# Two mixture-of-experts layers behind a long convolution: two second-layer sums to a PSUM bank, a third table of slots, and another order of items

## The chip, the cores and the metric

The kernel runs on one NeuronCore of a Trainium2 chip. The metric is the device time of one execution in microseconds; the median of three runs before the change is 1368.7 (1364.27 to 1370.17). TensorE is called PE, its weight loads PEld, VectorE DVE, ScalarE ACT, GpSimd POOL, and SyncE SP, whose queue issues most plain DMAs. DMAs with an index per row (gathers and scatters) are issued on POOL.

## The reference

```python
X = np.fft.rfft(x, axis=1)                       # x: 4 x 2496 x 256
y = np.fft.irfft(X * (filt_r + 1j * filt_i), n=2496, axis=1)
# layer 1: x = y as 9984 tokens of 256; 8 experts, 1248 tokens each
logits = x @ w_gate
# tokens and experts are paired greedily, best logit first, until an expert is full
h = np.maximum(x[mask] @ w1[e], 0.0); out[mask] = h @ w2[e]      # 256 -> 1024 -> 256
# layer 2: x = out; cosine similarity to 8 expert embeddings over tau
logits = xn @ en.T / tau
expert_idx = np.argmax(logits, axis=1)           # any number of tokens per expert
gate_w = softmax(logits)[expert_idx]
out[mask] = gate_w[mask, None] * (np.maximum(x[mask] @ w1[e], 0.0) @ w2[e])
```

## The kernel before

The convolution fills the first 250 us or so and leaves the tokens in DRAM (`xs`) and the first gate's logits in SBUF. From there on the kernel is one list of items (`plan`, line 1418), worked through by `layers` (line 1548).

An item is up to 512 tokens of one expert, in tiles of 128. Its columns are transposed on PE (L995) during the item before, at that item's fourth and sixth chunk of eight. The first matmuls (`l1`, L1012) run in eight chunks of 128 hidden columns, six matmuls each, since every operand is split into a high and a low part: ACT takes the high part of a sum (`k_hh`, L1015), DVE the rest (`k_hl`, L1018). The second matmuls (`l2`) follow two chunks behind. Weights are loaded on SP's queue (L940, L950), ACT rounds them to the high part and DVE or POOL subtracts for the low part (L957, L958); `engs` of a set says which of the two.

There are first-layer items and second-layer items ("slots"). First-layer items come in groups: the first full expert, then seven "known" experts in four groups, then seven "late" ones in three groups, a late item being the last 480 tokens of an expert. The greedy pairing (`search`), the lists of tokens (`listing`) and the routing of each finished group (`routes`) run as generators beside the matmuls. A group's `route` computes the second gate for its tiles (square sums on ACT, Newton steps on POOL, the rest on DVE and one small pair of matmuls, L1376 and L1377) and scatters the rows (the tiles `k_y`, 26 buffers in all) by POOL into `ys`, a DRAM region per second-layer expert.

A slot is 512 rows of one expert's region in `ys`. Which expert and which rows are in a table computed on DVE: `slA` (8 slots, only whole ones) when the last known group is routed, `slB` (12 slots) and `slS` (2 half slots) when all are. Behind the last table `pads` writes padding rows with sixteen scatters before the last two kinds of slots may be read. A slot's rows come on SP's queue (L1217). Slots beyond the static ones would run in a loop at the end (`rest`).

The order of instructions on each engine is fixed while the program is built: `beside` (line 1619) advances a model of the engines' times and lets each generator go on when its time has come; lists are asked before routes, and routes before the greedy pairing. Where `layers` needs a thing that isn't there yet, `need` (line 1585) issues all that is missing at once.

In a slot's second matmuls the high and low weights stand side by side, and a tile has two matmuls per chunk into one PSUM bank of 512 columns:

```python
nc.tensor.matmul(p[:m], hh[:, t0:t0 + m], W[0][:, f, :], start=f == 0, stop=False)
nc.tensor.matmul(p[:m, 0:256], hl[:, t0:t0 + m], W[0][:, f, 0:256], start=False, stop=f == 7)
```

A first-layer tile has three of 264 columns (L1029). A slot's tile leaves by a scaling on ACT (L1499) and a scaled addition on DVE (L1502), and POOL scatters it to `out` (L1409). Four banks (`kp_b`) hold the sums of one item.

Of the kernel before, what the change touches and what calls it, by code (L numbers as in the profile page):

```python
# [34 lines left out]
TS2 = 256  # L35
# [14 lines left out]
AFIRST = 5  # L50
# [867 lines left out]
class Core:  # L918
# [51 lines left out]
    def split2(s, raws, gated, engs, late=None):  # L970

        w = s.t([128, 2 * 8 * 264], F32R, "w2", 2)
        if gated:
            n = 264 if gated == 2 else 256
            W = [w[:, 2112 * k:2112 * k + 2112].rearrange("p (f d) -> p f d", f=8) for k in range(2)]
            H, L = W
        else:
            n = 256
            v = w[:, 0:4096].rearrange("p (f a d) -> p f a d", f=8, a=2)
            W = [w[:, 0:4096].rearrange("p (f d) -> p f d", f=8)]  # L980
            H, L = v[:, :, 0], v[:, :, 1]
        for h in range(2):
            a, b = (x[:, 4 * h:4 * h + 4, 0:n] for x in (H, L))
            s.part(a, b, raws[h].rearrange("p (f d) -> p f d", f=4)[:, :, 0:n], engs[h], late)
            yield W
# [35 lines left out]
    def l2(s, W, H, f, sums, ns):  # L1021

        nc = s.nc
        hh, hl = H[f]
        for b, (p, m) in enumerate(zip(sums, ns)):
            t0 = 128 * b
            if len(W) == 2:
                for q, (h, w) in enumerate(((hh, W[0]), (hh, W[1]), (hl, W[0]))):
                    nc.tensor.matmul(p[:m, :264], h[:, t0:t0 + m], w[:, f, :], start=f == 0 and q == 0, stop=f == 7 and q == 2)  # L1029
            else:  # L1030

                nc.tensor.matmul(p[:m], hh[:, t0:t0 + m], W[0][:, f, :], start=f == 0, stop=False)  # L1032
                nc.tensor.matmul(p[:m, 0:256], hl[:, t0:t0 + m], W[0][:, f, 0:256], start=False, stop=f == 7)  # L1033
# [3 lines left out]
class Moe:  # L1037
# [3 lines left out]
    NB = 12  # L1041
# [41 lines left out]
    def prep(s, w2tp):  # L1083

        nc, c, d = s.nc, s.c, s.d
        V = nc.vector
        s.run = s.t([128, 8], F32, "run")
# [132 lines left out]
    def routes(s):  # L1220
        for g in range(s.groups):
# [4 lines left out]
            if g == s.certain - 1:  # L1226
                s.table_a()
# [65 lines left out]
    def table_a(s):  # L1293
        c, V = s.c, s.nc.vector
        nt = s.count(c['base'], 0, 9)
        pl = s.t([128, 8], F32, "pla")
        V.tensor_scalar(pl, c['base'], 1.0 / TS2, None, op0=ALU.mult)
        s.slA, cum = s.table(nt, pl, 2, s.NA, "a")
        tk = s.t([128, 8], F32, "taken")

        V.tensor_tensor(tk, cum, nt, ALU.subtract)
        V.tensor_scalar(tk, tk, -1.0, float(s.NA), op0=ALU.mult, op1=ALU.add)
        V.tensor_scalar(tk, tk, 0.0, None, op0=ALU.max)
        V.tensor_tensor(tk, tk, nt, ALU.min)
        s.taken = tk
# [109 lines left out]
    def plan(s):  # L1415
# [16 lines left out]
        def place(name, k):  # L1432
            def f():
                yield from s.table_ready(name if name == 'slA' else 'padded')
# [529 lines left out]
```

## Time and profile before

| | |
|---|---|
| median of three runs | 1368.7 us |
| profiled execution | 1369.25 us |
| its span | 1367.5 us |
| PE busy | 1227.4 us (90%), 7221 matmuls |
| weight loads | 1028.8 us (75%) |
| DVE, ACT, POOL busy | 815.8, 662.7, 589.3 us |
| mean granted clock of TensorE | 0.96 of full speed |
| DMA | 178.26 MB, mean 130 GB/s |

Times in the trace count from the start of the span. Busy time of PE is pipelined: matmuls overlap, so the step from one to the next says what one costs. A wait is put down to what released the engine last. A window's row gives the busy time and the number of instructions of each engine in that stretch.

### The profile page before, as it was taken

How to read it: one execution, taken by the hardware profiler on the slowest of the kernel's cores; microseconds unless marked ns; L12 is line 12 of the kernel's file. 1: busy time of each engine (PE TensorE's matmuls, PEld its weight loads, DVE VectorE, ACT ScalarE, POOL GpSimd, SP SyncE). 2: the span in 40 equal slices, each digit the busy share in tenths (PEclk: the TensorE clock that was granted, in tenths of full speed). 3: DMA queues.
4: the chain of work that ended last, by engine and by line, in shares of the span. 5: the costliest groups of instructions: out<-in, count | busy, mean ns of one | idle time of the engine just before them, and what ended most of it. 6: DMA issues, size and time to landing. Idle time of an engine off the chain costs nothing. (4 is left out here: it accounts for less than half of the span.)

```text
span 1367.5 us, 22297 instructions
## 1 busy us (share of the span) xinstructions
PE 1227.4 (90%) x7221; PEld 1028.8 (75%) x7221; DVE 815.8 (60%) x2014; ACT 662.7 (48%) x1406; POOL 589.3 (43%) x1023
## 2 busy tenths in 40 slices
PE   8888999798998999997599989999828999999996
PEld 7555545688998989986588779988716888888885
DVE  3579676677879878797596656453612333333332
ACT  2566565454554646554264445554313444444442
POOL 1345200322454713663225324058773565565644
PEclk9999999999999999999799999999968999999998
DMA  8867486422232422320544334334144443444430
GB/s 238 257 231 227 157 264 230 146 85 66 80 95 67 138 76 87 101 75 15 175 143 154 108 111 140 109 100 133 61 161 130 140 131 128 142 134 129 127 103 24
DMA packets 124047, 178.26 MB, mean 130 GB/s; under 512 B 29383, under 2 KB 88763, under 8 KB 123645
## 3 DMA queue, kind: packets, MB, share of 16 engines
q1 hardware_dynamic: 111131, 143.33, 34.4%
q0 software_dynamic: 12480, 33.17, 7.2%
q8 instruction: 61, 1.00, 0.3%
q14 instruction: 85, 0.70, 0.2%
q10 hardware_dynamic: 290, 0.07, 0.0%
HBM read 137.32 MB, written 39.99 MB: 130 GB/s over the span
## 5 line engine op out<-in xcount | busy, mean ns | idle before, releaser
L1018 DVE SCALAR_TENSOR_TENSOR k_hl<-kp_a,k_hh 128x512 fp32r<-128x512 f32 (+3 forms) x368 | 229.1, 624 | 334.8 <-ACT k_hh L1015 297.3
L1015 ACT ACTIVATE k_hh<-kp_a 128x512 fp32r<-128x512 f32 (+3 forms) x368 | 201.4, 547 | 460.1 <-PE kp_a L1012 395.1
L1012 PE MATMUL kp_a<-k_xh,k_w1h 128*128 128x512 f32 (+3 forms) x736 | 278.1, 379 | 8.0 <-DVE k_hl L1018 5.3
L1012 PE MATMUL kp_a<-k_xl,k_w1h 128*128 128x512 f32 (+3 forms) x736 | 275.7, 375 | 0.0
L1032 PE MATMUL kp_b<-k_w,k_hh 128*128 128x512 f32 x672 | 253.6, 408 | 8.7 <-DVE k_xg L1502 8.4
L1029 PE MATMUL kp_b<-k_w,k_hh 128*128 128x264 f32 (+1 forms) x1280 | 254.1, 293 | 1.5 <-ACT k_y L1481 1.4
L1029 PEld LDWEIGHTS kp_b<-k_w,k_hh 128*128 128x128 f32 (+1 forms) x1280 | 204.9, 188 | 8.5 <-ACT k_y L1481 2.3
L1012 PE MATMUL kp_a<-k_xh,k_w1l 128*128 128x512 f32 (+3 forms) x736 | 211.2, 368 | 0.0
L1033 PE MATMUL kp_b<-k_w,k_hl 128*128 128x256 f32 x672 | 191.4, 285 | 3.5 <-DVE k_hl L1018 3.5
L1029 PE MATMUL kp_b<-k_w,k_hl 128*128 128x264 f32 (+1 forms) x640 | 182.7, 285 | 2.5 <-DVE k_hl L1018 2.5
L1012 PEld LDWEIGHTS kp_a<-k_xh,k_w1h 128*128 128x128 f32 x736 | 140.9, 191 | 30.4 <-DVE k_hl L1018 8.0
L1032 PEld LDWEIGHTS kp_b<-k_w,k_hh 128*128 128x128 f32 x672 | 128.7, 191 | 37.8 <-DVE k_xg L1502 9.7
L1012 PEld LDWEIGHTS kp_a<-k_xh,k_w1l 128*128 128x128 f32 x736 | 137.4, 190 | 18.8
L1012 PEld LDWEIGHTS kp_a<-k_xl,k_w1h 128*128 128x128 f32 x736 | 140.8, 191 | 10.0 <-DVE k_xl L998 0.3
L1208 POOL DMA_INDIRECT k_xg<-xs,g_ids x80 | 82.0, 1025 | 148.5 <-DVE w2r L1132 78.8
L1033 PEld LDWEIGHTS kp_b<-k_w,k_hl 128*128 128x128 f32 x672 | 128.6, 191 | 9.0 <-DVE k_hl L1018 3.9
L958 POOL TENSOR_TENSOR k_w1l<-k_raw,k_w1h 128x1024 fp32r<-128x1024 f32 x34 | 82.0, 2413 | 118.2 <-ACT k_w1h L957 118.1
L1409 POOL DMA_INDIRECT out<-k_xg,k_y x84 | 83.1, 989 | 94.2 <-DVE k_xg L1502 75.7
L1029 PEld LDWEIGHTS kp_b<-k_w,k_hl 128*128 128x128 f32 (+1 forms) x640 | 119.7, 187 | 3.0 <-DVE k_hl L1018 2.9
L1409 POOL DMA_INDIRECT ys<-k_y,m_pi x80 | 82.3, 1028 | 40.2 <-POOL m_sp L1408 16.9
L998 DVE TENSOR_TENSOR k_xl<-kp_a,k_xh 128x512 fp32r<-128x512 f32 (+3 forms) x92 | 57.0, 619 | 60.7 <-ACT k_xh L997 46.2
L303 POOL TENSOR_TENSOR v<-sw,ff 128x512 f32<-128x512 f32 x40 | 51.5, 1287 | 95.4 <-ACT sw L301 93.6
(340 smaller groups left out, 1896.5 us busy)
## 6 DMA issues: line engine op xcount, KB each, us to landing
k_raw<-w1n SPq DMA_DIRECT2D x44, 512.0 KB
k_raw<-w2n SPq DMA_DIRECT2D x44, 512.0 KB
k_raw<-w1m SPq DMA_DIRECT2D x30, 512.0 KB
k_raw<-w2m SPq DMA_DIRECT2D x30, 512.0 KB
k_y<-ys SPq DMA_DIRECT2D x84, 132.0 KB
ff<-ff SPq DMA_DIRECT2D x40, 256.0 KB
xs<-yt SPq DMA_DIRECT2D x42, 234.0 KB
w2m<-w2mt SPq DMA_DIRECT2D x16, 512.0 KB
```

The costliest lines, as they stand in the source:

```text
L303: nc.gpsimd.tensor_tensor(r2(v), r2(sw), bc(ff[:, 256:512]), ALU.mult)
L958: f = lambda: eng.tensor_tensor(lo, src, hi.bitcast(F32), ALU.subtract)
L998: late(lambda: nc.vector.tensor_tensor(b, p[:, :T], a.bitcast(F32), ALU.subtract), T)
L1012: nc.tensor.matmul(p[:, :T], w[:, c, f0:f0 + 128], x[:, c, :T], start=q == 0, stop=q == 5)
L1015: nc.scalar.activation(hh[:, :T], p[:, :T], AF.Relu)
L1018: nc.vector.scalar_tensor_tensor(o, a, 0.0, b, op0=ALU.max, op1=ALU.subtract), T, (id(H), f))
L1029: nc.tensor.matmul(p[:m, :264], h[:, t0:t0 + m], w[:, f, :], start=f == 0 and q == 0, stop=f == 7 and q == 2)
L1032: nc.tensor.matmul(p[:m], hh[:, t0:t0 + m], W[0][:, f, :], start=f == 0, stop=False)
L1033: nc.tensor.matmul(p[:m, 0:256], hl[:, t0:t0 + m], W[0][:, f, 0:256], start=False, stop=f == 7)
L1208: s.nc.gpsimd.indirect_dma_start(out=x[:m], out_offset=None, in_=s.d['xs'], in_offset=bass.IndirectOffsetOnAxis(ap=ids[:m], axis=0))
L1409: st = s.nc.gpsimd.indirect_dma_start(out=out, out_offset=bass.IndirectOffsetOnAxis(ap=idx, axis=0), in_=src, in_offset=None, **k)
```

## The change

In a slot, high and low weights now stand apart as in the first layer, and each tile and chunk has three matmuls of 256 columns (high by high, high by low, low by high) that sum into 256 columns. Two tiles share a bank, so a slot takes two of the four banks. The exit is one scaling on ACT for each tile, issued for both tiles behind the second one's last matmul, and the scatter is issued at once.

The late experts are grouped (1, 2, 3), (4, 5), (6, 7) instead of (1, 2), (3, 4, 5), (6, 7). Three late items come ahead of the first slot instead of two. A third table `slM` of 3 whole slots is computed when the group (4, 5) is routed; `slB` has 9 slots instead of 12. The order is now: known groups, late 1 to 3, four slots, late 4 and 5, three slots, late 6 and 7, one slot, three slots of `slM`, nine of `slB`, two half slots. Before: known groups, late 1 and 2, five slots, late 3 to 7, three slots, twelve, two half ones. Seven slots instead of five have their weights' low part on DVE. Routes are asked before lists.

```diff
-            if len(W) == 2:
-                for q, (h, w) in enumerate(((hh, W[0]), (hh, W[1]), (hl, W[0]))):
-                    nc.tensor.matmul(p[:m, :264], h[:, t0:t0 + m], w[:, f, :], start=f == 0 and q == 0, stop=f == 7 and q == 2)
-            else:
-
-                nc.tensor.matmul(p[:m], hh[:, t0:t0 + m], W[0][:, f, :], start=f == 0, stop=False)
-                nc.tensor.matmul(p[:m, 0:256], hl[:, t0:t0 + m], W[0][:, f, 0:256], start=False, stop=f == 7)
+            n = W[0].shape[2]
+            for q, (h, w) in enumerate(((hh, W[0]), (hh, W[1]), (hl, W[0]))):
+                nc.tensor.matmul(p[:m, :n], h[:, t0:t0 + m], w[:, f, :], start=f == 0 and q == 0 and (n > 256 or b % 2 == 0),
+                                 stop=f == 7 and q == 2 and (n > 256 or b % 2 == 1))
...
-    NB = 12
+    NM = 3
+    NB = 9
...
-            if g == s.certain - 1:
-                s.table_a()
+            if g in s.tables:
+                s.table_a(*s.tables[g])
                 yield 3.5
...
-        late = [[(("late", k), (LATE,)) for k in q] for q in ((1, 2), (3, 4, 5), (6, 7))]
+        late = [[(("late", k), (LATE,)) for k in q] for q in ((1, 2, 3), (4, 5), (6, 7))]
...
+        s.tables = {len(full + known) - 1: ('slA', s.NA), len(full + known) + 1: ('slM', s.NM)}
         first(late[:1])
-        slots('slA', range(AFIRST), 4, (V, V))
-        first(late[1:])
-        slots('slA', range(AFIRST, s.NA), 4, (P, P))
+        slots('slA', range(4), 4, (V, V))
+        first(late[1:2])
+        slots('slA', range(4, 7), 4, (V, V))
+        first(late[2:])
+        slots('slA', range(7, s.NA), 4, (P, P))
+        slots('slM', range(s.NM), 4, (P, P))
         slots('slB', range(s.NB), 4, (P, P))
...
-            nc.scalar.activation(o, p[:, 0:256], AF.Copy, scale=y[:, 257:258])
-
-            def g():
-                nc.vector.scalar_tensor_tensor(o, p[:, 256:512], y[:, 257:258], o, op0=ALU.mult, op1=ALU.add)
-                s.scatter('out', s.out, y[:, 256:257].bitcast(I32), o, bounds_check=NTOK - 1, oob_is_err=False)
-            late(g)
+            s.nc.scalar.activation(o, p[:, 0:256], AF.Copy, scale=y[:, 257:258])
+            s.on_act(0.38, s.pe)
+            s.scatter('out', s.out, y[:, 256:257].bitcast(I32), o, bounds_check=NTOK - 1, oob_is_err=False)
...
+    def sums(s, z, first):
+        if first:
+            return [s.k.P([128, 512], "b", 4) for _ in z['n']]
+        two = [s.k.P([128, 2, 256], "b", 4) for _ in z['n'][::2]]
+        return [two[b // 2][:, b % 2] for b in range(len(z['n']))]
...
-                else:
-                    s.done2(z, b, lambda h: s.push(s.on_act(0.38, s.pe) + 0.1, h, None, 0.4))(z['sums'][b])
+                elif b % 2:
+                    for a in (b - 1, b):
+                        s.done2(z, a)(z['sums'][a])
...
-        for n, room in (('lists', ROOM), ('routes', ROOM), ('greedy', GROOM)):
+        for n, room in (('routes', ROOM), ('lists', ROOM), ('greedy', GROOM)):
```

## Rows read from the trace of the kernel before

**Rows 1.** Page, part 2: slices, TensorE's busy tenths and granted clock.
```profile
PE   8888999798998999997599989999828999999996
...
PEclk9999999999999999999799999999968999999998
```

**Rows 2.** Waits of PE: line, what for; us in total, times, longest.
```profile
PE kp_a L995 <- DMA k_y<-ys: 46.3, 4, 30.1
PE pr L1376 <- DVE m_M L1372: 12.1, 3, 6.6
PE kp_b L1032 <- DVE k_xg L1502: 8.4, 3, 4.7
...
PE kp_a L995 <- DMA k_xg<-xs,g_ids: 6.1, 3, 4.6
...
PE kp_b L1033 <- DVE k_hl L1018: 3.5, 1, 3.5
```

**Rows 3.** Windows: length, busy us (count) of five engines, clock, DMA share, GB/s.
```profile
1057.76:1174.65 116.89, 116.89 (x602) 98.05 (x601) 41.74 (x70) 53.91 (x89) 69.00 (x61) 1.00 0.44 135
869.79:892.76 22.97, 22.97 (x154) 21.47 (x152) 11.52 (x16) 12.38 (x26) 1.54 (x11) 1.00 0.43 117
616.64:664.15 47.51, 24.33 (x161) 21.72 (x159) 28.18 (x110) 14.51 (x43) 18.43 (x64) 0.80 0.09 32
664.15:892.76 228.61, 219.35 (x1247) 189.37 (x1247) 149.03 (x328) 114.33 (x233) 64.80 (x144) 0.97 0.45 138
739.27:798.95 59.68, 51.62 (x247) 42.09 (x246) 36.10 (x82) 22.61 (x38) 26.31 (x48) 0.91 0.40 121
892.76:920.01 27.25, 24.59 (x155) 22.70 (x154) 17.45 (x33) 13.01 (x26) 13.19 (x32) 0.94 0.33 104
971.95:1030.64 58.69, 25.08 (x121) 20.50 (x119) 18.29 (x67) 11.58 (x19) 42.60 (x77) 0.74 0.36 123
1030.64:1057.76 27.12, 26.76 (x121) 21.75 (x122) 7.70 (x13) 10.47 (x17) 10.22 (x9) 0.87 0.47 138
```

**Rows 4.** Timeline of PE, second layer: start us, us; first layer's triples, slot's pairs.
```profile
617.44 0.40 PE L1029 MATMUL kp_b<-k_w,k_hh 128*128 128x264 f32 x2
...
617.80 0.40 PE L1029 MATMUL kp_b<-k_w,k_hh 128*128 128x264 f32 x2
...
1070.22 0.39 PE L1032 MATMUL kp_b<-k_w,k_hh 128*128 128x512 f32 x1
...
1070.57 0.40 PE L1032 MATMUL kp_b<-k_w,k_hh 128*128 128x512 f32 x1
```

**Rows 5.** Groups of instructions, 1057.76 to 1291.58, ten slots: busy us, mean ns.
```profile
L1033 PEld LDWEIGHTS kp_b<-k_w,k_hl 128*128 128x128 f32 x320 | 60.1, 188 | 2.7
...
L958 POOL TENSOR_TENSOR k_w<-k_raw,k_w 128x1024 fp32r<-128x1024 f32 x20 | 47.6, 2404 | 3.0 <-ACT k_w L957 2.1 <-issue 0.8
L1409 POOL DMA_INDIRECT out<-k_xg,k_y x41 | 40.2, 980 | 16.3 <-DVE k_xg L1502 7.3 <-issue 6.8 <-DVE k_hl L1018 2.3
...
L1502 DVE SCALAR_TENSOR_TENSOR k_xg<-kp_b,k_y,k_xg 128x256 f32<-128x256 f32 x40 | 16.5, 476 | 0.0
```

**Rows 6.** Timeline of PE, transposes of the second late item and first slot.
```profile
616.64 0.57 PE L995 MATMUL kp_a<-ident,k_xg 128*128 128x128 f32 x4
...
664.15 0.48 PE L995 MATMUL kp_a<-ident,k_y 128*128 128x128 f32 x1 [15.76 <-DMA k_y<-ys]
```

**Rows 7.** Timeline of SP's queue around the fifth slot's rows.
```profile
730.96 2.61 SPq L1217 DMA_DIRECT2D k_y<-ys  x4
```

**Rows 8.** Timelines of ACT, POOL and PE along the last chain.
```profile
938.24 1.39 ACT L1481 COPY k_y<-kp_b 128x264 f32<-128x264 f32 x4
...
994.72 0.98 POOL L1409 DMA_INDIRECT ys<-m_fill,m_pzi  x1 [6.08 <-DVE m_pzi L1241]
...
1025.88 0.96 POOL L1409 DMA_INDIRECT ys<-m_fill,m_pzi  x1 [0.22 <-issue]
...
1030.64 1.09 PE L995 MATMUL kp_a<-ident,k_y 128*128 128x128 f32 x2 [30.10 <-DMA k_y<-ys]
```

More of the change, by code (lines that the diff above doesn't have):

```diff
@@ L49 @@
 BEHIND = 2
-AFIRST = 5
 GROOM = 1.5
@@ L972, in split2 @@
         w = s.t([128, 2 * 8 * 264], F32R, "w2", 2)
[L973 to L976, printed above, removed]
-        else:
[L978 to L981, printed above, removed]
+        n = 264 if gated == 2 else 256
+        m = 8 * (264 if gated else 256)
+        W = [w[:, m * k:m * k + m].rearrange("p (f d) -> p f d", f=8) for k in range(2)]
         for h in range(2):
-            a, b = (x[:, 4 * h:4 * h + 4, 0:n] for x in (H, L))
+            a, b = (x[:, 4 * h:4 * h + 4, 0:n] for x in W)
             s.part(a, b, raws[h].rearrange("p (f d) -> p f d", f=4)[:, :, 0:n], engs[h], late)
@@ L1086, in prep @@
         V = nc.vector
+        s.taken = s.t([128, 8], F32, "taken")
+        V.memset(s.taken, 0.0)
         s.run = s.t([128, 8], F32, "run")
@@ L1291, in count, with table_a @@
         return nt
-    def table_a(s):
+    def table_a(s, name, N):
         c, V = s.c, s.nc.vector
-        nt = s.count(c['base'], 0, 9)
+        sub = s.t([128, 8], F32, "sub")
+        V.scalar_tensor_tensor(sub, s.taken, 512.0, c['base'], op0=ALU.mult, op1=ALU.add)
+        nt = s.count(sub, 0, 9)
         pl = s.t([128, 8], F32, "pla")
-        V.tensor_scalar(pl, c['base'], 1.0 / TS2, None, op0=ALU.mult)
-        s.slA, cum = s.table(nt, pl, 2, s.NA, "a")
-        tk = s.t([128, 8], F32, "taken")
+        V.tensor_scalar(pl, sub, 1.0 / TS2, None, op0=ALU.mult)
+        sl, cum = s.table(nt, pl, 2, N, name)
+        tk = s.t([128, 8], F32, "takn")
         V.tensor_tensor(tk, cum, nt, ALU.subtract)
-        V.tensor_scalar(tk, tk, -1.0, float(s.NA), op0=ALU.mult, op1=ALU.add)
+        V.tensor_scalar(tk, tk, -1.0, float(N), op0=ALU.mult, op1=ALU.add)
         V.tensor_scalar(tk, tk, 0.0, None, op0=ALU.max)
         V.tensor_tensor(tk, tk, nt, ALU.min)
-        s.taken = tk
+        V.tensor_tensor(s.taken, s.taken, tk, ALU.add)
+        setattr(s, name, sl)
     def table_b(s):
@@ L1433, in f @@
             def f():
-                yield from s.table_ready(name if name == 'slA' else 'padded')
+                yield from s.table_ready('padded' if name in ('slB', 'slS') else name)
                 return getattr(s, name), k
@@ L1526, in second @@
             s.need('weights2', lambda: 'W2' in Z)
-            z['sums'] = [s.k.P([128, 512], "b", 4) for _ in z['n']]
+            z['sums'] = s.sums(z, first)
             if first:
@@ L1740, in alone @@
         H = []
-        sums = [k.P([128, 512], "b", 4) for _ in z['n']]
+        sums = s.sums(z, w2x is not None)
         one = k.l1(W1, X, H)
```

6 lines of the change are left out of this document (1 added, 5 removed).

## The prediction

> **What bounds the kernel now.** I read the page's slices first, then the waits of PE, then windows between dated PE events. The slices [rows 1] show PE at nine tenths nearly everywhere, with two holes: slices 19 and 20 (counted from 1), and slice 30, where PE is busy two tenths and the granted clock falls to six tenths (1.2 GHz for part of it). So this is a PE kernel with two stalls, and a change is worth what it takes out of the stalls or out of the matmuls. The waits name the holes [rows 2]: transposes of slot rows (L995, reading k_y) waited 46.3 us in four waits, 30.1 the longest; route matmuls (L1376) 12.1 in three, 6.6 the longest; L1032 waited 8.4 for the DVE exit L1502.
>
> The windows give what an item costs when nothing is late [rows 3]: five slots in 116.89 us with PE busy all of it, 23.38 each; one late item 22.97. Against these, 616.64 to 664.15 (one late item's worth) lost 47.51 - 22.97 = 24.5; 664.15 to 892.76 (five slots, four late items, 208.8 at those prices) lost 19.8, of which 739.27 to 798.95 has 59.68 - 46.76 = 12.9; 892.76 to 920.01 lost 4.3; 971.95 to 1030.64 lost 35.3; the slot after it 3.7, at a granted clock of 0.87. Some 88 us between 616 and 1058 is all that can be won by order; from 1058 on only a cheaper slot would help.
>
> **The change, part by part.**
>
> *Three matmuls in place of two.* A second-layer slot tile now has three 256-wide matmuls where it had a 512 and a 256: the same 768 columns and one more weight load. There are 20 x 32 + 2 x 16 = 672 such tile steps. The pair takes 0.35 us from L1032 to the next L1032; the first layer's triple, of the new shape at 264 columns, takes 0.36 [rows 4]. Scaled by 256/264 that is 0.349; unscaled 0.36 is the upper end. So -0.7 to +6.7 us; I take +1, nearest the scaled triple.
>
> At this place a rule of the Trainium skill speaks against the change: "TensorE: Matmul & The Clock Gate", Part 3, The mechanism, says that a weight load overlaps matmuls in flight only when its row group differs, and here all loads are 128 by 128. With that page's 107 ns for 128 columns (an estimate), 672 loads would add 72 us. The triple's 0.36 us for three loads and 792 columns does not agree with it, so it stays a rival.
>
> *The exit.* ACT scales both tiles after the second is summed; the DVE addition (476 ns, [rows 5]) goes, 84 times, 40 us of DVE. ACT's work per tile stays. The scatter is issued straight behind it, so POOL stands behind ACT instead of DVE; what queues there (weight subtractions, route scatters) waits no longer than now. A slot holds two of four banks, so the next slot's sums don't wait for this one's exits. In the steady slots PE has no wait to lose, so nothing is gained there. Where it did wait, 739 to 799, L1502 stood behind DVE's weight subtractions and a greedy phase; the 12.9 us there are L1032's 8.4 us of wait [rows 2], which fall in this stretch, and the lower clock after each. DVE stays late, and then k_hl (L1018) is late next, with two chunks of slack; I leave 4 of 12.9. Bounds: 0 to 12.9 left.
>
> *A third late item ahead of the first slot.* The first slot's rows wait for the route of the last known group, its scatters and the table. Late item two is transposed at 616.64, the slot rows land at 664.15 [rows 6]. With item three between, PE reaches the slot's transposes at 616.64 + 2 x 22.97 = 662.6. If the chain of route, scatters and table keeps its date, 1.6 is left; I take 2, so slot zero starts at 664.6 without the half clock that followed the long wait. Below: an unforced route could be 3 earlier, which gains nothing; above: 8 later.
>
> What rides along: four gathers on POOL, one more set of first-layer weights on SP and its DVE subtraction, all moved from later. Group five now keeps twelve k_y tiles instead of eight of 26 until its scatters. Before, SP's load of slot four's rows went out at 730.96 [rows 7], beside those scatters; now slot three's (transposed at about 664.6 + 70 = 735) meets the same point, and the weight loads queue behind it on SP. I keep 4 us for this and for the routes' matmul waits (5.5 in two waits, [rows 2]) that stay. Bounds 0 to 20.
>
> *Sets moved from POOL to DVE.* Two more slots have their subtractions on DVE: eight, 2.4 us each on POOL [rows 5]. POOL gets 19 us back, DVE at most as much; the vanished exits of these sets pay part of it. Cost 0, bounds 0 to 5, inside the 8 left for this stretch.
>
> *The table in between.* One more call of some thirty small DVE instructions behind group six, four slots or more ahead of its first reader: hidden. If that cover were gone, the wait would be a whole route chain, as below.
>
> *Routes polled first.* Lists and greedy phases go behind a route on DVE. Gathered rows made PE wait 6.1 us in three waits [rows 2]. I take 0, bounds -3 to +8. It does nothing in the tail, where no list or phase is left.
>
> *Three slots ahead of the last table.* Before, the last late item's sums leave PSUM at 938.24; squares, route, eight scatters, table, sixteen padding scatters (994.72 to 1025.88), and slot rows are transposed at 1030.64 [rows 8]: a chain of 92.4 us. PE had run until 1030.64 - 30.1 = 1000.5, that is 62.3, of which some 2.8 (one of the two shorter L1376 waits) and 3.5 are waits inside [rows 2] and about 1 low clock (an estimate from them): 55 us of work. One more slot stands between now: 55 + 23.4 = 78. So 14 us of the stall should stay, with about 3.7 of half clock behind it, against 35.3 + 3.7. The chain's own length: POOL does weight subtractions and output scatters between its links; with PE running on, more fall in, 2.4 and 1.0 us each [rows 5], but the route's links are unchanged. Bounds 78 (all covered) to 112; I take 92.4.
>
> **The sum, in dates.** Slot zero 664.6. To the seventh late item: seven slots and three late items, 7 x 23.38 + 3 x 22.97 = 232.6, plus 8 lost: 905.2. To its exit: before 938.24 - 892.76 = 45.5, less the 4.3 lost in it, 41.2: 946.4. Chain 92.4: 1038.8. From the first last-table slot to the end of the span before: 1367.5 - 1030.64 = 336.9; three slots fewer (70.1): 266.7. That is 1305.5, plus 1 for the triples: 1306.5. The profiled execution took 1369.25 for a span of 1367.5, so 1308; it stands 0.55 above the median of 1368.7, which I ignore.
>
> **Rivals.**
> 1. *The last chain is covered.* If the route's links tighten (no DVE exit ahead of POOL), 14 us and the half clock go: 1308 - 18 = 1290. For it: POOL idled 6.08 us before the padding scatters [rows 8]. Against it: each link waits for the one before, and POOL's other work grows.
> 2. *The chain stretches.* POOL, 69.0 of 116.9 us busy in steady slots [rows 3], interleaves the route with three running slots: chain 112, 1308 + 20 = 1328.
> 3. *New waits among slots one to six:* k_hl behind DVE's subtractions, SP behind k_y tiles. 20 to 25 more: 1330.
> 4. *The weight loads are not hidden* (the other side). A load takes 188 ns [rows 5], longer than a 256-wide matmul's step of 0.12. Exposed in full, 672 x 0.188 = 126: 1434. It undoes the 61 us gained from 91 ns a load on. Against it: the triple of [rows 4].
> 5. *It doesn't do what it says:* the middle table finds fewer than three whole slots, and as many run empty and come back in the overflow loop at the end. Each costs 23 empty and at least two half slots of 12 us of matmul with 9.6 of exposed subtraction, some 66: 1374 with one. Against it: counting the reference's second gate on its inputs gives 14 whole slots, remainders 62, 214, 385 and up; the 960 tokens of the two last late lists can take away three at most, leaving 8 + 3.
>
> **Chances.** Forecast 0.62, rival 1 0.14, rival 2 0.12, rival 3 0.05, rival 4 0.03, rival 5 0.04. The forecast alone spans 1296 to 1322. The range reaches from rival 1 with an idle middle, 1284, to rivals 2 and 3 with part of the 20 of the k_y tiles, 1338. About 0.5%, 7 us, is what a measurement tells here: faster 0.92, same 0.03 (rival 5 with one slot), slower 0.05.
>
> **What would show it.** The slot zero transposes near 664 with a wait below 5 us where 22 stood; no wait on a DVE exit; PE waiting 10 to 20 us, not 30, ahead of the first last-table slot, and that at 1035 to 1043; steady slots of 23.3 to 23.7. A steady slot over 24.5 would make the forecast wrong by the matmuls, a last wait over 30 by the chain.

## The result, and the profile after

| | before | after |
|---|---|---|
| median | 1366.5 us (4 runs, 1357.4 to 1370.2) | 1317.7 us (4 runs, 1313.7 to 1320.3) |
| profiled execution, its span | 1369.25, 1367.5 us | 1320.3, 1318.4 us |
| PE busy | 1227.4 us (90%), 7221 matmuls | 1222.3 us (93%), 7893 matmuls |
| weight loads | 1028.8 us (75%) | 1060.2 us (80%) |
| DVE, ACT, POOL busy | 815.8, 662.7, 589.3 us | 787.2, 663.0, 571.9 us |

The ratio of the times is 0.965 (95% interval 0.9595 to 0.9705), some 48 us less. It lies 10 us above the forecast of 1308, within its range. Lines have moved: the transposes (L995 before) are L988, `l1` L1005, `k_hl` L1011, `l2` L1023, weight rounding and subtraction L956 and L957, the slot rows' load L1211, POOL's scatters L1407.

The page of the changed kernel, part 2; it answers to [rows 1].

```profile
PE   8988999799999999999969989999998899999995
...
PEclk9998999899999999999989999999998999999998
```

The hole of slice 30 is gone. One slice (21, the stretch from 659 to 692 us) is still at six tenths, at a lowered clock. The waits of PE (in total, times, longest) say what that is; they answer to [rows 2].

```profile
PE kp_a L1005 <- DVE k_hl L1011: 24.4, 11, 10.0
...
PE kp_a L988 <- DMA k_y<-ys: 5.3, 2, 5.0
PE kp_b L1023 <- DVE k_hl L1011: 4.8, 2, 3.8
...
PE pr L1374 <- DVE m_M L1370: 1.3, 1, 1.3
```

Waits for slot rows went from 46.3 us to 5.3, for the route's masks from 12.1 to 1.3, and none names a DVE exit any more. In their place stands a wait that the profile before did not have: 10.0 us for `k_hl`. The windows between first transposes price it; the columns are those of [rows 3].

```profile
663.01:700.01 37.00, 26.68 (x162) 23.90 (x161) 24.17 (x55) 16.37 (x34) 1.41 (x4) 0.86 0.55 174
773.39:802.12 28.73, 25.41 (x161) 23.06 (x160) 14.75 (x37) 10.92 (x23) 5.19 (x10) 0.94 0.42 123
663.01:919.45 256.44, 241.99 (x1561) 218.85 (x1560) 165.00 (x385) 126.28 (x252) 89.78 (x203) 0.97 0.46 142
990.84:1020.71 29.87, 26.11 (x154) 23.40 (x152) 15.96 (x62) 11.05 (x18) 24.97 (x46) 0.89 0.34 111
1049.70:1076.67 26.97, 26.79 (x152) 23.54 (x153) 6.13 (x9) 9.64 (x16) 17.68 (x21) 0.88 0.64 196
1100.17:1264.84 164.67, 164.67 (x1066) 149.35 (x1065) 47.75 (x70) 77.49 (x126) 96.23 (x85) 1.00 0.42 130
```

From slot zero's transposes (663.01) to the next slot's 37.00 us pass where a slot costs 23.38 [rows 3]: 13.6 lost, 10.0 of them the wait, the rest at a granted clock of 0.86. It is more than half of what is lost between 663.01 and the seventh late item at 919.45, 256.44 - 232.6 = 23.8. The timeline around it shows how the wait comes about (start, duration, engine, line, operation, and in brackets the engine's idle time and what ended it).

```profile
658.08 1.21 DVE L1011 SCALAR_TENSOR_TENSOR k_hl<-kp_a,k_hh 128x480 fp32r<-128x480 f32 x2
667.34 1.22 DVE L957 TENSOR_TENSOR k_w1l<-k_raw,k_w1h 128x1024 fp32r<-128x1024 f32 x1 [8.04 <-ACT k_w1h L956]
...
675.00 0.15 DVE L801 TENSOR_SCALAR g_ei<-g_rst 128x1 int32<-128x1 f32 x1 [4.55 <-DVEq L794]
675.07 0.65 DVE L1011 SCALAR_TENSOR_TENSOR k_hl<-kp_a,k_hh 128x480 fp32r<-128x480 f32 x1
...
666.26 1.04 ACT L956 CAST k_w1h<-k_raw 128x1024 fp32r<-128x1024 f32 x1 [6.62 <-DMA k_raw<-w1n]
667.21 0.56 ACT L1008 ACTIVATE k_hh<-kp_a 128x480 fp32r<-128x480 f32 x1
...
659.92 2.07 SPq L1211 DMA_DIRECT2D k_y<-ys  x4
662.83 0.91 SPq L939 DMA_DIRECT2D k_raw<-w1n  x2
...
663.99 0.33 PE L988 MATMUL kp_a<-ident,k_y 128*128 128x128 f32 x1 [0.31 <-DMA k_y<-ys]
...
675.78 0.77 PE L1005 MATMUL kp_a<-k_xh,k_w1h 128*128 128x480 f32 x1 [10.01 <-DVE k_hl L1011]
```

Read it from below. Slot zero's rows come in time (0.31 us of wait). On SP they went out at 659.92, when the last scatters had landed, and slot zero's first weights stand behind them, at 662.83. ACT is to round these weights ahead of the third late item's next `k_hh`, whose sum was done at 660.4, and waits 6.62 us for them; DVE is to subtract them ahead of that item's `k_hl`, and waits 8.04. Of the two it is ACT's wait that counts, since that `k_hh` itself ended only at 667.77. Behind the subtraction the greedy phase reads a register and branches on it (L793, L794): 4.55 us in which DVE does nothing, most of it behind the branch (last section). So a `k_hl` whose sum was done long before runs at 675.07, and PE needs its bank.

### The profile page after: what moved, and what is told of

The parts are those of the page before. It is cut to its first block, busy times and chain, and to the rows that moved or that the text cites. A ratio compares the mean times of both kernels' runs of the same rounds, so it can differ in the third digit from the quotient of the medians.

```text
span 1318.4 us, 23498 instructions
## 1 busy us (share of the span) xinstructions
PE 1222.3 (93%) x7893; PEld 1060.2 (80%) x7893; DVE 787.2 (60%) x1969; ACT 663.0 (50%) x1406; POOL 571.9 (43%) x1015
## 5 line engine op out<-in xcount | busy, mean ns | idle before, releaser
L1023 PE MATMUL kp_b<-k_w,k_hh 128*128 128x256 f32 (+2 forms) x2624 | 509.6, 290 | 2.0 <-ACT k_y L1481 2.0
L1023 PEld LDWEIGHTS kp_b<-k_w,k_hh 128*128 128x128 f32 (+1 forms) x2624 | 422.2, 189 | 16.4 <-ACT k_y L1481 2.9
L1011 DVE SCALAR_TENSOR_TENSOR k_hl<-kp_a,k_hh 128x512 fp32r<-128x512 f32 (+3 forms) x368 | 228.7, 624 | 337.5 <-ACT k_hh L1008 295.7
L1023 PE MATMUL kp_b<-k_w,k_hl 128*128 128x256 f32 (+2 forms) x1312 | 374.3, 285 | 4.8 <-DVE k_hl L1011 4.8
L1005 PE MATMUL kp_a<-k_xh,k_w1h 128*128 128x512 f32 (+3 forms) x736 | 274.9, 374 | 26.3 <-DVE k_hl L1011 24.4
L1005 PE MATMUL kp_a<-k_xl,k_w1h 128*128 128x512 f32 (+3 forms) x736 | 273.2, 372 | 0.0
L1023 PEld LDWEIGHTS kp_b<-k_w,k_hl 128*128 128x128 f32 (+1 forms) x1312 | 248.0, 189 | 5.3 <-DVE k_hl L1011 5.2
L1005 PE MATMUL kp_a<-k_xh,k_w1l 128*128 128x512 f32 (+3 forms) x736 | 212.8, 370 | 0.1
L1005 PEld LDWEIGHTS kp_a<-k_xh,k_w1h 128*128 128x128 f32 x736 | 140.3, 191 | 39.3 <-DVE k_hl L1011 27.4
L1005 PEld LDWEIGHTS kp_a<-k_xh,k_w1l 128*128 128x128 f32 x736 | 137.3, 190 | 16.8
L1005 PEld LDWEIGHTS kp_a<-k_xl,k_w1h 128*128 128x128 f32 x736 | 139.9, 190 | 9.9 <-issue 0.4
L1407 POOL DMA_INDIRECT out<-k_xg,k_y x84 | 84.2, 1002 | 96.3 <-ACT k_xg L1498 79.4
L957 POOL TENSOR_TENSOR k_w1l<-k_raw,k_w1h 128x1024 fp32r<-128x1024 f32 x30 | 71.9, 2401 | 105.7 <-ACT k_w1h L956 105.6
L1407 POOL DMA_INDIRECT ys<-k_y,m_pi x80 | 82.8, 1035 | 34.0 <-POOL m_sp L1406 16.3
L1482 POOL COPY m_L<-k_y 128x8 f32<-128x8 f32 x80 | 18.1, 248 | 150.1 <-ACT k_y L1481 148.8
L956 ACT CAST k_w1h<-k_raw 128x1024 fp32r<-128x1024 f32 x74 | 76.9, 1042 | 6.6 <-DMA k_raw<-w1n 6.6
L956 ACT CAST k_w<-k_raw 128x1024 fp32r<-128x1024 f32 (+2 forms) x75 | 78.4, 1048 | 0.9 <-DMA k_raw<-w2n 0.9
L957 POOL TENSOR_TENSOR k_w<-k_raw,k_w 128x1024 fp32r<-128x1024 f32 x30 | 71.5, 2401 | 14.9 <-ACT k_w L956 13.8
```

Source lines behind the costliest of these rows:

```text
L956: s.nc.scalar.copy(hi, src)
L957: f = lambda: eng.tensor_tensor(lo, src, hi.bitcast(F32), ALU.subtract)
L1005: nc.tensor.matmul(p[:, :T], w[:, c, f0:f0 + 128], x[:, c, :T], start=q == 0, stop=q == 5)
L1011: nc.vector.scalar_tensor_tensor(o, a, 0.0, b, op0=ALU.max, op1=ALU.subtract), T, (id(H), f))
L1023: nc.tensor.matmul(p[:m, :n], h[:, t0:t0 + m], w[:, f, :], start=f == 0 and q == 0 and (n > 256 or b % 2 == 0), stop=f == 7 and q == 2 and ...
L1407: st = s.nc.gpsimd.indirect_dma_start(out=out, out_offset=bass.IndirectOffsetOnAxis(ap=idx, axis=0), in_=src, in_offset=None, **k)
```

## The experiments

The ratio is to the kernel before, timed beside each on the same chip (its medians there were 1359.9 for e1 to e4, 1365.1 for e5 to e8 and 1365.4 for the other four), so ratios are compared, not medians. Line numbers of these kernels differ by a few.

| run | edit | median us | ratio, 95% interval |
|---|---|---|---|
| the change | | 1317.7 | 0.965 [0.9595, 0.9705] |
| e1_sums | only the sums and the exit | 1348.9 | 0.992 [0.9897, 0.9944] |
| e2_order | all but the sums and the exit | 1322.4 | 0.9728 [0.9711, 0.9744] |
| e3_poll | lists asked first again | 1314.9 | 0.9669 [0.9653, 0.9685] |
| e4_two | without the third table | 1332.0 | 0.9793 [0.9762, 0.9824] |
| e12_late2 | two late items ahead, not three | 1340.4 | 0.9798 [0.9767, 0.9829] |
| e5_early | slot zero's weights ahead of its rows | 1308.9 | 0.960 [0.9555, 0.9646] |
| e6_place | their rounding and subtraction placed later | 1311.3 | 0.9619 [0.9563, 0.9675] |
| e7_pool | their subtraction on POOL | 1314.6 | 0.9635 [0.9589, 0.9681] |
| e10_hold | greedy phase held back there | 1309.8 | 0.9575 [0.9543, 0.9607] |
| e8_tail | one slot more behind the last late item | 1310.5 | 0.9605 [0.9559, 0.9651] |
| e9_both | e5 and e8 | 1306.4 | 0.9563 [0.9537, 0.9588] |
| e11_all | first weights, rows, second weights on SP; held; tail | 1300.7 | 0.9535 [0.9498, 0.9571] |

### The change in two halves

e1_sums keeps the new `l2`, `split2`, `sums` and `done2`, and takes back the rest:

```diff
-    NM = 3
-    NB = 9
+    NM = 0
+    NB = 12
...
-        late = [[(("late", k), (LATE,)) for k in q] for q in ((1, 2, 3), (4, 5), (6, 7))]
+        late = [[(("late", k), (LATE,)) for k in q] for q in ((1, 2), (3, 4, 5), (6, 7))]
...
+        slots('slA', range(5), 4, (V, V))
+        first(late[1:])
+        slots('slA', range(5, s.NA), 4, (P, P))
...
-        for n, room in (('routes', ROOM), ('lists', ROOM), ('greedy', GROOM)):
+        for n, room in (('lists', ROOM), ('routes', ROOM), ('greedy', GROOM)):
```

> The kernel before with one part of the change alone: three 256-wide matmuls per slot tile and chunk, two tiles to a bank, the exit by one scaling. Order of items, tables and polling as before. Theory (the exits were a wait, the matmuls cost next to nothing): PE's waits for the DVE exit (8.4 us in three) are gone, a steady slot costs 23.5 instead of 23.38 us (about +3 over 20 slots), so 1366 - 9 - some half clock + 3 = about 1358 us. Rival A (DVE stays late and k_hl takes the exit's place): waits for k_hl of about the same length in the stretch of the first slots, 1366 to 1369 us. Rival B (fewer bytes behind DVE also shorten the last chain): 1345 or less, with the last wait for slot rows below 25 us instead of 30.1.

e2_order is the other half: the functions `split2`, `l2`, `done2` and the sums' banks as before, all else as changed.

```diff
...
-                elif b % 2:
-                    for a in (b - 1, b):
-                        s.done2(z, a)(z['sums'][a])
+                else:
+                    s.done2(z, b, lambda h: s.push(s.on_act(0.38, s.pe) + 0.1, h, None, 0.4))(z['sums'][b])
...
```

> The changed kernel with the old second matmuls (512 and 256 columns, one bank per tile) and the old exit with DVE's scaled addition; the order of items, the third table and the polling stay changed. Theory (the order is worth about 40 of the 49 us): 1324 to 1330 us, with PE waiting again for the DVE exit (5 to 10 us) somewhere between the first slot and the last late item. Rival (the parts don't add up: without the exit's DVE work the order could not have paid): 1340 or more, with the 10.0 us wait for k_hl behind slot zero grown to over 15.

Measured: 0.992 and 0.9728. Their product is 0.965, the ratio of the whole change: 0.8% or 11 us from the sums, 2.7% or 37 from the order. So the halves add, within the interval of the change, some 7 us either way; 2 to 3 us in each half are the faster pace of the last table's slots told of at the end. First two windows of e1, nine steady slots and the stretch from slot three to the third late item; then seven steady slots of e2; then e2's waits of PE between 600 and 1100 us.

```profile
1063.44:1271.93 208.49, 208.49 (x1370) 190.07 (x1369) 61.31 (x90) 98.67 (x161) 123.55 (x109) 1.00 0.44 135
736.80:786.00 49.20, 47.89 (x318) 42.94 (x317) 33.70 (x88) 23.01 (x43) 23.27 (x36) 1.00 0.48 148
```

```profile
1105.54:1267.68 162.14, 162.14 (x842) 137.11 (x841) 58.74 (x98) 76.74 (x126) 96.50 (x85) 1.00 0.43 132
```

```profile
PE kp_a L1011 <- DVE k_hl L1017: 10.8, 2, 10.0
...
PE kp_b L1031 <- DVE k_xg L1510: 5.9, 4, 2.1
...
PE kp_b L1028 <- DVE k_xg L1510: 1.9, 1, 1.9
```

208.49 / 9 = 23.17 us for a slot with three matmuls, 162.14 / 7 = 23.16 with two. So the third weight load costs nothing that shows: kernels with the same matmuls differ by up to 0.36 us a slot (last section), and 32 loads of 188 ns [rows 5] laid bare would be 6.0. With the old exit 7.8 us of waits for it are back, and the 10.0 us wait behind slot zero is there too: it belongs to the order, not to the sums. In e1 the stretch where the exits were waited for takes 49.20 us where the kernel before took 59.68 [rows 3]; one wait of 1.3 for `k_hl` is left in it. So the exit's theory held: 10.5 us there and 11 in all, for some 8 expected. Rival A fell, and B too: the last wait for rows is 27.3 us in e1, against 30.1.

### What the order did

e3_poll swaps the two names back in `beside`.

> The changed kernel with lists asked before routes, as before the change. Theory (the poll order moves nothing that PE waits for): within 4 us of the changed kernel's 1317.7, the 10.0 us wait for k_hl behind slot zero included. Rival (routes first is what keeps slot zero's table at its date): slot zero's rows land 3 to 8 us later, PE waits for them, 1321 to 1326. Rival the other way (routes first pushes the greedy phase with its register read to behind slot zero's weights, and that is the 10 us wait): the wait shrinks and the time falls by 5 to 12, to 1306 to 1313.

The time is the same (0.9669 against 0.965), but for a reason that the theory did not have. PE's row of slot zero's transposes, and two of DVE ahead of it:

```profile
653.47 0.15 DVE L801 TENSOR_SCALAR g_ei<-g_rst 128x1 int32<-128x1 f32 x1 [3.49 <-DVEq L794]
...
664.93 0.17 DVE L1273 CAST m_slslA<-m_tk 128x8 int32<-128x8 f32 x1
...
673.61 0.44 PE L988 MATMUL kp_a<-ident,k_y 128*128 128x128 f32 x1 [11.07 <-DMA k_y<-ys]
```

Now the greedy phase with its register read goes first, and the table is ready at 664.93 instead of 657.1; PE waits 11.07 us for rows instead of 10.01 for `k_hl`. That is the first rival's mechanism, while the wait that it replaces is gone. The wait changes its name and hardly its size: DVE has more to do between the last known group's sums and slot zero than one late item covers. What the windows say besides is that the equal time is two differences that cancel: from the third late item's transposes to slot one's 64.78 us pass, 60.58 in the change, and from late four's to late five's 24.47, in the change 28.73.

e4_two takes the third table out: one slot of `slA` between late 5 and late 6, three behind late 7, twelve of `slB`.

```diff
...
-        slots('slA', range(4, 7), 4, (V, V))
+        slots('slA', range(4, 5), 4, (V, V))
         first(late[2:])
-        slots('slA', range(7, s.NA), 4, (P, P))
-        slots('slM', range(s.NM), 4, (P, P))
+        slots('slA', range(5, s.NA), 4, (P, P))
...
```

> The changed kernel without the third table: known groups, late 1 to 3, four slots, late 4 and 5, one slot, late 6 and 7, three slots, then twelve slots from the last table. One slot fewer stands between the last late item and the last table than in the changed kernel. Theory (the chain from the last late item's exit to the padded rows has its own length, about 89 to 92 us, and every slot put beside it takes 23.4 us out of the stall): the wait for the first last-table slot's rows grows from 5.0 to about 28 us, 1317.7 + 23 to 26 = 1341 to 1344. Rival (the chain's length grows and shrinks with what runs beside it, so the cover buys less): the wait grows by 12 or less, 1326 to 1332.

```profile
908.53 1.36 ACT L1480 COPY k_y<-kp_b 128x264 f32<-128x264 f32 x4
...
997.56 1.45 PE L988 MATMUL kp_a<-ident,k_y 128*128 128x128 f32 x3 [27.28 <-DMA k_y<-ys]
```

The wait grew from 4.96 to 27.28 us, by 22.3, one slot; from the last late item's exit to the transposes 997.56 - 908.53 = 89.0 us pass, as in the changed kernel (below: 88.9). With less beside it the chain keeps its length, as the theory said; with one slot more it grows (e8 below). By the ratios the time rose by 1.5% (0.9793 / 0.965), 20 us, a little under the 23 to 26 expected; e4 ran its last table's slots at the faster pace told of at the end.

e12_late2 regroups the late experts, with two ahead of slot zero.

```diff
-        late = [[(("late", k), (LATE,)) for k in q] for q in ((1, 2, 3), (4, 5), (6, 7))]
+        late = [[(("late", k), (LATE,)) for k in q] for q in ((1, 2), (3, 4, 5), (6, 7))]
```

> The changed kernel with the late experts in groups of two, three and two as before, so that two late items, not three, come ahead of slot zero. Theory (the route chain in front of slot zero keeps its date, the third item covers it): PE waits about 16 us for slot zero's rows (15.9 where only the sums were changed), the 10.0 us wait for k_hl behind it shrinks since DVE catches up meanwhile; net about +10 to +16, 1328 to 1334. Rival (the third item only moved the loss from PE's rows to DVE's queue, total the same): 1315 to 1322.

```profile
662.07 0.47 PE L988 MATMUL kp_a<-ident,k_y 128*128 128x128 f32 x1 [21.19 <-DMA k_y<-ys]
```

```profile
737.50:770.90 33.40, 28.62 (x157) 23.80 (x155) 19.59 (x35) 13.50 (x22) 9.82 (x15) 0.85 0.37 103
```

The first row is of PE's timeline, the second a window. The wait for rows is back, at 662.07, the date at which they land with three items ahead too (663): the third item covers 23 us of a chain that keeps its date. The time is above what was expected, 1.5% more than the change's. The excess lies in the window 737.50 to 770.90, an item with 33.40 us and a clock of 0.85. In it PE stood six times between 740 and 748, 0.4 to 1.2 us each and 4.7 in all, for nothing that the profile shows, and ran at half clock from 743 to 753. The cause stays open.

### The wait behind slot zero

Four edits take one thing each out of it. e5_early sends slot zero's weight loads ahead of its rows on SP; the rows' generator waits for them:

```diff
...
                 sl, k = yield from z['place']()
+                while n == s.slot0 and s.sent < 2 and not s.force:
+                    yield 1
...
```

> The changed kernel with slot zero's weight loads issued on SP's queue ahead of its row loads instead of behind them. Theory (the 10.0 us wait for k_hl behind slot zero comes from its first weights: the row loads wait on SP for the last scatters until 659.9, the weights behind them are issued at 662.8 and land at 666.3, ACT's rounding and DVE's subtraction of them stand ahead of late item three's k_hh and k_hl): the weights land about 5 us earlier, the wait falls from 10.0 to about 5, the time by 5 to 8, to 1310 to 1313. Rival (it is the register read of 4.55 us that the greedy phase makes on DVE between the two): k_hl keeps its date or moves by no more than 1 us after DVE has waited elsewhere, 1316 to 1319.

e6_place lets `weights1` wait eight steps instead of four between slot zero's load and its rounding:

```diff
-            yield 8 if z['w2x'] is not None else 4
+            yield 8 if z['w2x'] is not None or z['i0'] == s.slot0 else 4
...
```

> The changed kernel with slot zero's roundings and subtractions of first weights issued some 5 us later in the order of instructions (after eight steps of the generator instead of four); loads unchanged. Theory (as in the run before): ACT and DVE no longer stand behind weights that have not landed; the greedy phase with its register read runs at once and k_hl comes at about 667 instead of 675. The 10.0 us wait falls to 0 to 3, the half clock behind it goes, 1317.7 minus 8 to 13 = 1305 to 1310. Rival (the work on DVE there is too much wherever it stands): the wait comes back one chunk later or at slot zero's first matmuls for its weights, 6 us or more of it, 1313 to 1318.

e7_pool gives slot zero's set to POOL:

```diff
-        slots('slA', range(4), 4, (V, V))
+        slots('slA', range(1), 4, (P, P))
+        slots('slA', range(1, 4), 4, (V, V))
```

> The changed kernel with slot zero's low parts subtracted on POOL instead of DVE. Theory: DVE's part of the wait goes and ACT's stays (k_hh behind the rounding until 667.2): k_hl at about 668 to 670 instead of 675, the wait falls from 10.0 to 3 to 5 us, the time by 6 to 9, to 1309 to 1312. Rival (POOL's subtractions at 2.4 us each come too late for slot zero's first matmuls, or hold up the scatters of the next route): a new wait of PE for k_w1l or for slot rows of 3 us or more, 1315 to 1322.

e10_hold keeps the greedy pairing from going on during the third late item:

```diff
...
             q = s.bg[n]
+            if n == 'greedy' and s.it == s.slot0 - 1:
+                continue
```

> The changed kernel with the greedy pairing kept from going on while late item three's first matmuls run, so that its register read (4.55 us of DVE there) comes behind slot zero's weights; loads and weights unchanged. Theory (the 10.0 us wait for k_hl is made of two things in a row: ACT and DVE standing behind slot zero's first weights until 668.5, then the greedy phase with its read until 675): the wait falls by the second part, 6.5, to 3 to 4 us, 1317.7 - 6 to 8 = about 1311. Rival (the weights alone set it): the wait stays at 9 or more, 1316 to 1319. Rival (the read only moves): another wait for k_hl of 4 us or more appears later, while slot zero runs.

PE's rows of the wait in e5, e6, e7 and e10, in this order:

```profile
667.36 1.51 PE L988 MATMUL kp_a<-ident,k_y 128*128 128x128 f32 x4 [3.93 <-DMA k_y<-ys]
```

```profile
671.36 0.77 PE L1005 MATMUL kp_a<-k_xh,k_w1h 128*128 128x480 f32 x1 [4.27 <-DVE k_hl L1011]
```

```profile
671.11 0.77 PE L1005 MATMUL kp_a<-k_xh,k_w1h 128*128 128x480 f32 x1 [5.06 <-DVE k_hl L1011]
```

```profile
668.79 0.77 PE L1005 MATMUL kp_a<-k_xh,k_w1h 128*128 128x480 f32 x1 [3.71 <-DVE k_hl L1011]
```

Each cuts the wait from 10.0 to about 4 or 5, but a shorter wait is not yet a shorter stretch: from the third late item's transposes to slot one's the change takes 60.58 us, e5 54.07, e6 54.44, e10 53.70 and e7 61.14. In e5 the weights land earlier, DVE's subtraction starts at 663.05 instead of 667.34, and a wait for the rows (now third in SP's queue, sent at 662.30) of 3.93 comes up, as was not expected; the time fell by 0.5% or 7 us, of 5 to 8 expected. In e6 ACT stands behind slot zero's second weights instead (7.93 us), half the rival, but the `k_hh` that PE needs is done before that, at 662.96; its `k_hl` comes at 670.64 because DVE stands still for 3.34 us behind the branch and, one instruction later, for 3.48 more. In e7 ACT's part is left, 2.5 us of wait come up further on, and the stretch is no shorter than the change's. The 2.5 us have a cause that was not expected: two small instructions of the greedy phase on DVE take ten times their length, while POOL subtracts slot zero's weights (673.52 to 678.26).

```profile
673.74 2.19 DVE L809 TENSOR_SCALAR g_oh<-c_rev,g_rst 128x8 f32<-128x8 f32 x1
```

That one ends within 0.03 us of POOL's subtraction beside it, and the next, L811 with 2.44 us, within 0.03 of the following one; without a subtraction beside them (e5) both take 0.22 and 0.23. So e7's time, 0.9635 against 0.965, shows no gain. In e10 the read is gone from there, and the wait falls by 6.3, of 6.5 expected; the read now ends at 689, during slot zero's matmuls, with no wait of PE beside it. The greedy phases behind it move too: slots one to three take 78.24 us against 73.38, with waits for `k_hl` of 0.7, 1.9 and 1.1, and from late four's transposes to late five's 23.56 pass against 28.73. So the wait is two things in a row, weights that come late and a branch on DVE, and either alone leaves about 4 us (e6, e10). The intervals of these four overlap one another; the stretches tell them apart from the changed kernel better than the times do.

### The tail, and all together

e8_tail moves one slot of `slA` from ahead of late 6 to behind late 7.

```diff
-        slots('slA', range(4, 7), 4, (V, V))
+        slots('slA', range(4, 6), 4, (V, V))
         first(late[2:])
-        slots('slA', range(7, s.NA), 4, (P, P))
+        slots('slA', range(6, s.NA), 4, (P, P))
```

> The changed kernel with one more slot of the first table behind the last late item (six of the first table before it instead of seven; that slot's subtractions move from DVE to POOL). Theory (the last chain has its own length of about 89 us and was short of cover by the 5.0 us wait): the wait for the first last-table slot's rows goes to 0, and the low clock of the slot after it (3.5 us) too: 1317.7 - 8 = about 1310. Rival (the chain stretches with more slots beside it, through POOL's subtractions between its links): the wait stays at 3 to 8 us, 1315 to 1320. Rival (the route of late 4 and 5 or the third table is now short of cover): a new wait for slot rows ahead of slot zero of the third table, slower than 1320.

The rows of the changed kernel's chain, and then those of e8: the exit of the last late item, the padding scatters (the first and the last; of e8 the last), the first last-table slot's transposes.

```profile
960.76 1.37 ACT L1481 COPY k_y<-kp_b 128x264 f32<-128x264 f32 x4
...
1011.13 0.98 POOL L1407 DMA_INDIRECT ys<-m_fill,m_pzi  x1 [2.13 <-DVE m_pzi L1235]
1044.71 0.96 POOL L1407 DMA_INDIRECT ys<-m_fill,m_pzi  x1 [0.23 <-issue]
...
1049.70 1.45 PE L988 MATMUL kp_a<-ident,k_y 128*128 128x128 f32 x3 [4.96 <-DMA k_y<-ys]
```

```profile
937.67 1.37 ACT L1481 COPY k_y<-kp_b 128x264 f32<-128x264 f32 x4
...
1028.38 0.96 POOL L1407 DMA_INDIRECT ys<-m_fill,m_pzi  x1 [0.23 <-issue]
...
1047.38 0.60 PE L988 MATMUL kp_a<-ident,k_y 128*128 128x128 f32 x4
```

The wait is gone, and the ratio is 0.5% lower, some 6 us, though the two intervals overlap. The chain did stretch, from 84.0 to 90.7 us up to the last padding scatter, as the first rival had it, but rows are there some 5 us behind that scatter (1044.71 to 1049.70 in the change), and PE came 19 us behind it.

e9_both is e5 and e8 in one:

> The changed kernel with the two edits that helped alone: slot zero's weight loads ahead of its rows (measured alone: 1308.9 against 1365.1 of before in the same call, ratio 0.960) and one slot more behind the last late item (1310.5, ratio 0.9605). Theory (the two losses lie 300 us apart and don't touch): both gains add, about 8 + 7 off 1317.7, 1302 to 1305, ratio 0.955. Rival (the tail's cover had been spent already by the earlier start): less than 3 us better than either alone, 1306 or more.

0.9563, where 0.960 and 0.9605 give 0.9555 if both gains add to the change's 0.965: they add, within the intervals.

e11_all puts the first weights, then the rows, then the second weights on SP, holds the greedy phase as in e10, and has e8's tail:

```diff
...
+            while z['i0'] == s.slot0 and not s.items[s.slot0]['x'] and not s.force:
+                yield 1
             raws = s.k.load2(nc.sync, nc.sync.value_load(ei, min_val=0, max_val=7), z['w2'], z['w2x'])
...
+                while n == s.slot0 and s.sent < 1 and not s.force:
+                    yield 1
...
```

> The changed kernel with three edits: on SP slot zero's first weights, then its rows, then its second weights; the greedy pairing held while late item three's first matmuls run; one slot more behind the last late item. Theory: slot zero's rows land as early as in the changed kernel (no wait), neither the weights nor the register read stand ahead of k_hl for long, so the 13.6 us lost around slot zero fall to 0 to 4, and the tail's 8 go: 1317.7 - 18 to 21 = 1297 to 1300, ratio 0.950 to 0.952. Rival (DVE has too much to do between the last known group's route and slot zero, and the wait only moves again): 5 us or more of new waits for k_hl or for late rows between 665 and 800, 1303 to 1308.

Its windows from the third late item's transposes to slot zero's, and from those to the next slot's:

```profile
634.63:659.53 24.90, 23.54 (x156) 21.44 (x155) 19.25 (x70) 10.73 (x25) 9.41 (x31) 1.00 0.28 97
659.53:684.30 24.77, 24.50 (x155) 21.85 (x156) 13.20 (x27) 13.46 (x28) 1.78 (x4) 1.00 0.56 178
```

37.00 has become 24.77, and the first theory holds around slot zero; 0.9535 is a little short of the 0.950 to 0.952 expected. As in e10, waits for `k_hl` of 0.7, 1.9 and 1.1 us came up in the three slots behind (76.69 us, 73.38 in the change), and from late four's transposes to late five's 23.56 us pass instead of 28.73. With an interval of 0.9498 to 0.9571 it is the fastest version, 1.2% below the change, whose interval begins at 0.9595.

## Why the prediction was right, and which of its steps was off

The dates of the forecast against the profiled execution:

| step | forecast | measured |
|---|---|---|
| slot zero's transposes | 664.6 | 663.0 |
| lost from there to late seven | 8 | 23.8 |
| late seven to its exit | 41.2 | 960.76 - 919.45 = 41.3 |
| chain to the first last-table slot | 92.4 | 1049.70 - 960.76 = 88.9 |
| from there to the span's end | 267.7 | 1318.4 - 1049.7 = 268.7 |

The differences, -1.6, +15.8, +0.1, -3.5 and +1.0, make the 11.8 us by which the span is longer than the 1306.5 forecast. All but one are small. Of the signs that were named, slot zero's short wait, no wait on a DVE exit and steady slots of 23.5 us came; the last stall did not: 5.0 us at 1049.7 and not 10 to 20 at 1035 to 1043. That the chain's -3.5 made good part of the middle's +15.8 is luck. One sum of the prediction is short: its 88 us of loss leave out the two items from 920.01 to 971.95, 51.94 us for a price of 46.8, so some 93; no term of the forecast hangs on it.

*The third late item* did what was worked out: the rows landed within 2 us of the date, and e12 shows the same date with the wait back.

*The term that was mis-sized* is the 4 us "for this and for the routes' matmul waits", what rides along with the third item. Around slot zero 13.6 us were lost. The prediction looked for the cost in what moves with the third item, and on SP at slot three, where the kernel before had shown it; it had no term for slot zero's own set of weights, which was there before. That set meets three things at once: SP's queue, in which the weights stand behind rows that wait for scatters; the queues of ACT and DVE, in which their rounding and subtraction stand ahead of `k_hh` and `k_hl`; and the greedy phase's branch. In the kernel before neither the branch nor the weights stood in PE's way:

```profile
646.05 0.15 DVE L802 TENSOR_SCALAR g_ei<-g_rst 128x1 int32<-128x1 f32 x1 [3.27 <-DVEq L795]
...
667.93 0.91 SPq L940 DMA_DIRECT2D k_raw<-w1n  x2
...
671.46 1.05 ACT L957 CAST k_w1h<-k_raw 128x1024 fp32r<-128x1024 f32 x1 [0.50 <-DMA k_raw<-w1n]
```

The branch's 3.27 us lay inside PE's wait for the route, 6.59 us until 648.07, and the weights went out behind the stall for rows, with 0.50 us of ACT's wait. e12, with two items ahead, has that stall again and no wait for `k_hl` over 0.3 us around slot zero. So the stall of 24.5 us had covered them, or put them off. The Trainium skill states the rule that DVE's and ACT's queues are strict first in, first out ("PSUM — Partial Sum Buffer", section Engine vs sequencer instructions); the trace agrees, with ACT's 6.62 us wait of L956 ahead of a `k_hh` whose sum was done at 660.4. It is near rival 3 (k_hl behind DVE's subtractions) in another place; all told this stretch lost 15.8 us more than forecast, of its 20 to 25. Routes first, taken as 0, is 0 in e3 within the interval.

*The other 4 us*, DVE late where the exits were: from 773.39 to 802.12 28.73 us passed, 5.8 over a late item's price, again `k_hl` behind DVE (3.3 us of wait) and the clock of 0.94 behind it. "k_hl is late next" held, at 5.8 instead of 4, and what it stands behind is again the greedy phase's branch:

```profile
777.92 0.15 DVE L801 TENSOR_SCALAR g_ei<-g_rst 128x1 int32<-128x1 f32 x1 [4.83 <-DVEq L794]
```

Of the 23.8 us the rest is 3.2 in slots one to three and 1.2 between 802.12 and 919.45.

*The last chain* came out at 88.9 us of 92.4. 5.0 us of the stall stayed, not 14: the chain was 3.5 us shorter, with POOL idle for 2.13 us ahead of the padding scatters instead of 6.08 [rows 8], and the slots that cover it had lost time themselves, from the second slot of `slM` to the third 29.87 - 23.38 = 6.5 us, since the last table's small DVE instructions hold up a `k_hl` (a 3.8 us wait, then a clock of 0.89). The 3.7 of half clock stayed as forecast, 26.97 - 23.38 = 3.6. Rival 1 (covered by tighter links) came about in part only; e8 covered the chain with a slot.

*The matmuls.* The +1 for the triples is 0 in e1 against e2, as far as the pace of a program lets it be told. Rival 4 (exposed weight loads) is shut out: 32 loads more in a slot cost nothing in steady slots with 91% of the window under loads. By the sentence of the Trainium skill that the prediction draws on (the page and section named there) they could not overlap; the trace does not agree. Nor did rival 5 come about: had a slot of `slM` run empty, the tail would have been longer than forecast by tens of us, and it is 1.

## What to carry to other kernels

Where work is moved into a stall, ask what else ran in the stall's cover or was put off by it: loads, roundings and branches become the next wait, on engines whose queues run in order. Place an instruction that depends on a DMA behind the instructions that the bottleneck engine is about to need, or send its DMA first. If undoing an edit changes a wait's name and not its size (e3), the engine has too much to do in that stretch: move work out of it (e10, e11) or send its data earlier (e5). Judge an edit by the time of the stretch and not by the wait that it was aimed at: e7 halved the wait and gained nothing.

## What the hardware showed that was not expected

The last table's steady slots run at one pace in a program, and it differs from program to program, at a granted clock of 1.00 in all windows: 23.17 us a slot in e1, e2 and e4, 23.38 before, 164.67 / 7 = 23.52 in the change and in every run with its matmuls and its third table. PE alone differs. The groups of 1100 to 1250 us (busy, mean ns), of the change and of e4:

```profile
L1023 PE MATMUL kp_b<-k_w,k_hh 128*128 128x256 f32 x408 | 76.8, 286 | 0.0
...
L957 POOL TENSOR_TENSOR k_w1l<-k_raw,k_w1h 128x1024 fp32r<-128x1024 f32 x12 | 28.8, 2402 | 45.8 <-ACT k_w1h L956 45.8
```

```profile
L1023 PE MATMUL kp_b<-k_w,k_hh 128*128 128x256 f32 x416 | 76.8, 282 | 0.0
...
L957 POOL TENSOR_TENSOR k_w1l<-k_raw,k_w1h 128x1024 fp32r<-128x1024 f32 x14 | 33.6, 2397 | 52.5 <-ACT k_w1h L956 52.5
```

The same matmul takes 286 or 282 ns, the same POOL subtraction 2402 or 2397. e3, with the same steady slots, ran on e4's chip at 23.5, and e3 and e5 to e12, on three chips, agree to 0.02 us, so it goes with the program and not with the chip or the execution. Slots ahead of the last table are not all at that pace (23.30 from 825.79 to 849.09 in the change). Over the nine slots of the last table the 1.5% is some 3 us. Its cause stays open.

The register read and the branch behind it that the greedy phase makes on DVE (L793, L794) hold that engine for 3.3 to 4.8 us each time, 4.55 in the wait above, and DVE's busy time doesn't count it. The read is the small part. Its row in the changed kernel (ns, least, median and most), and the instruction queue's between the end of the branch, 670.90, and DVE's next record, 674.89 (packets, MB):

```profile
L793 DVEq TENSOR_LOAD <-g_fl x7: 314/323/552, 219.1 to 772.8; - x7
```

```profile
q14 instruction: 2, 0.02, 1.1%
```

Each of the 98 such branches in the 14 traces has a packet of 8 KB on that queue, begun 0.8 to 2.3 us behind the branch, and DVE goes on 1.2 to 2.5 us after the first one's end. That DVE waits there for its next instructions is inferred from this, and no run takes it away. e6 and e7 show the same once more one instruction later: packets at 668.80 and 668.55, and `k_hl` 1.5 us after their end.

Some of DVE's small instructions wait for POOL: behind the convolution the 14 traces have 37 instructions of DVE longer than 1.5 us (2.0 to 2.8, where their like take 0.2 to 0.3), and each ends within 0.13 us of the end of a subtraction of weights on POOL. Those that read a sum from PSUM (`k_hl`, `k_xl`) are not held: 25 of them run inside such subtractions in the change, in 0.4 to 0.7 us.
